# A batch's numerators inside a gate-and-value unit instead of behind it

## The chip, the cores and the metric

The kernel runs on one core of one Trainium2 chip. The metric is the time on the device, in microseconds, from the start to the end of one execution. A run gives one such time; the time of a kernel is the median of several runs. One further execution was taken with the hardware profiler: its span is the time from the first to the last instruction that it recorded. The engines are TensorE (PE, whose weight loads are listed as PEld), VectorE (DVE), ScalarE (ACT), GpSimd (POOL) and SyncE (SP), which here only issues transfers.

## What is computed

An attention with linear cost, and behind it a gated feed-forward block. Cut to what matters, with batch 8, heads 8, sequence 576, head size 64, and 4608 tokens of width 512 in the second part:

```python
def phi(x):                       # cos and sin of a position's angle
    r = np.maximum(x, 0)
    return np.concatenate([r * cos_w, r * sin_w], axis=-1)

q_p, k_p = phi(q), phi(k)         # (b, h, s, 128)
kv  = np.einsum('bhsf,bhsd->bhfd', k_p, v)
z   = k_p.sum(axis=2)
num = np.einsum('bhsf,bhfd->bhsd', q_p, kv)
den = np.einsum('bhsf,bhf->bhs', q_p, z)[..., None] + 1e-6
x   = (num / den).transpose(0, 2, 1, 3).reshape(4608, 512)
g   = x @ w_gate                  # (4608, 1536)
out = (0.5 * g * (1 + erf(g / sqrt(2))) * (x @ w_val)) @ w_out
```

## The kernel before

**The feed-forward part** goes over the tokens in nine blocks: block 0 has the 576 tokens of batch 0, blocks 1 to 7 have 512 each, block 8 has 448. A block's hidden layer of 1536 is cut into 12 units of 128. For each unit, `gate` runs four matmuls of 128x512 (one for each 128 of the width 512) into one PSUM bank, and ScalarE applies the GELU to it; `value` runs four matmuls into another bank, and VectorE multiplies both into `hT`. I call this the product (L233). The gate uses banks 0 and 1 in turn, the value part banks 2 and 3. The output tiles of a block (`o_tile`, twelve matmuls of 128x512 each) run during the next block, behind units 1, 3, 6 and 9, in banks 4 and 5; ScalarE copies the result out and SP stores it.

**The attention of batch n + 1** runs during block n, for n from 1 to 6. Batches 0 and 1 are handled ahead of that, and the change doesn't touch them. In the first units of a block, VectorE and ScalarE scale queries and keys and cast values; a transposing transfer on SP's queue turns the queries (`turn_q`). Then come six steps, `attn_step`, one per unit. Step 0 is the key-value sums: 40 small matmuls into banks 6 and 7 (`kv_half`), which ScalarE copies out to `kv`. Steps 1 to 5 handle 128 tokens each (the last one 64): eight small matmuls of 65 columns, the numerators with their denominators, into banks 6 and 7 (L169); then the normalization on VectorE, which is an addition (L181), a reciprocal (L183) and a multiplication (L184) into the tile `xb`; then a transposing transfer of `xb` into `xT` on SP's queue (`turn_x`, L204). The fifth goes to a tile `xr` first (L207), and POOL copies half of its columns into `xT` (L208). `xT` is what the gates and the value parts read, so a block's last steps feed the next block. Block 2 begins with tokens of batch 1 and reads the first four of batch 2's five parts.

**The order** is written out by hand. The program's order on each engine is the order in which the code issues instructions; nothing reorders them, and an instruction that waits holds up those behind it on its engine or queue. Semaphores are set by the framework from the tiles that instructions read and write. The lists `after[n][unit]` hold what follows a unit: for blocks 2 to 6 the loads of the batch after next stand behind units 3, 4 and 5, step 0 behind unit 5, and steps 1 to 5 behind units 6 to 10. In block 1 all steps are one unit earlier (step 0 behind unit 4, steps 1 to 5 behind units 5 to 9), and the loads stand behind units 5 (queries), 10 (keys) and 11 (values). Output tiles are appended to the same lists last, so behind units 6 and 9 the attention step comes first and the output tile second.

Two consecutive steps use the same two banks: the numerators of a step wait until the normalization of the step before has read them. The key-value sums of step 0 are in the same banks, and the first numerators read their copy, `kv`.

`gv_unit` has a parameter for functions to be called between the gate and the value part. No call in the kernel before uses it.

Of the kernel before, what the change touches and what calls it, by code (L numbers as in the profile page):

```python
# [16 lines left out]
def kernel(  # L17
# [18 lines left out]
    JT = J // 128  # L36
# [9 lines left out]
    NB = len(starts)  # L46
# [166 lines left out]
    def gate(n, jt, c0, w, gb):  # L213

        p0 = starts[n] + c0
        for ct in range(CT):
            nc.tensor.matmul(  # L217
                ps[:, gb, 0:w], lhsT=wg_sb[:, ct, jt * 128:(jt + 1) * 128],
                rhs=xT[:, ct, p0:p0 + w], start=(ct == 0), stop=(ct == CT - 1),
            )  # L220
        gels[n, jt, c0] = gel = rot.tile([128, 512], FP32, name="gel", bufs=3)
        nc.scalar.activation(gel[:, 0:w], ps[:, gb, 0:w], AF.Gelu)  # L222

    def value(n, jt, c0, w, vb):

        p0 = starts[n] + c0
        for ct in range(CT):
            nc.tensor.matmul(  # L228
                ps[:, vb, 0:w], lhsT=wv_sb[:, ct, jt * 128:(jt + 1) * 128],
                rhs=xT[:, ct, p0:p0 + w], start=(ct == 0), stop=(ct == CT - 1),  # L230
            )
        gel = gels.pop((n, jt, c0))
        nc.vector.tensor_mul(hT[n % 2][:, jt, 64 + c0:64 + c0 + w], gel[:, 0:w], ps[:, vb, 0:w])  # L233

    def gv_unit(n, jt, c0, w, gb, vb, mid=()):
        gate(n, jt, c0, w, gb)
        for f in mid:
            f()
        value(n, jt, c0, w, vb)

    def carry(n):

        w = ends[n] - starts[n]
        nc.gpsimd.tensor_copy(hT[(n + 1) % 2][:, :, 0:64], hT[n % 2][:, :, w:w + 64])  # L244
# [205 lines left out]
    def L(f, *a):  # L450
        return lambda: f(*a)
# [70 lines left out]


    after = {n: {jt: [] for jt in range(JT)} for n in range(NB)}
    for n in range(1, 7):
        b = n + 1
        a = after[n]

        def put(u, *fs):
            a[u].extend(fs)  # L530

        s = 0 if n > 1 else -1
        if n > 1:
            put(0, L(sq, 0, 0, "v"), L(sq, 1, 0, "v"), L(sq, 1, 1, "v"), L(sq, 0, 1, "s"))
            put(1, L(sq, 2, 0, "v"), L(sq, 2, 1, "s"), L(turn_q, b, 0, 3))
            put(1, L(sq, 3, 0, "v"), L(sq, 4, 0, "v"), L(sq, 4, 1, "v"), L(sq, 3, 1, "s"), L(turn_q, b, 3, 5))
        else:
            put(0, L(sq, 1, 1, "s"), L(sq, 2, 1, "v"), L(turn_q, b, 0, 3))
            put(0, L(sq, 3, 1, "v"), L(sq, 4, 1, "s"), L(turn_q, b, 3, 5))
        put(2 + s, L(sk, 0, 0, "v"), L(sk, 1, 0, "v"), L(sk, 0, 1, "s"), L(sk, 1, 1, "s"))  # L540
        put(3 + s, L(sk, 2, 0, "v"), L(sk, 3, 0, "v"), L(sk, 4, 0, "v"))
        put(3 + s, L(sk, 2, 1, "s"), L(sk, 3, 1, "s"), L(sk, 4, 1, "s"), L(cast_v, b, 0, 4))
        put(4 + s, L(cast_v, b, 4, 8, "s"))
        put(5 + s, L(attn_step, b, 0))
        if b + 1 < B:

            for f, u in zip((load_q, load_k, load_v), (3, 4, 5) if n > 1 else (5, 10, 11)):
                put(u, L(f, b + 1))
        for i in range(5):
            put(6 + s + i, L(attn_step, b, i + 1))  # L550

    for n in range(2, NB):
        for i, m in enumerate(o_tiles_of(n - 1)):
# [2 lines left out]
    def run_block(n):  # L556
        w = ends[n] - starts[n]
        for jt in range(JT):
            gv_unit(n, jt, 0, w, jt % 2, 2 + jt % 2)
            for f in after[n][jt]:  # L560
                f()
        if n + 1 < NB:
            carry(n)

    for n in range(1, NB):
        run_block(n)
# [34 lines left out]
```

## Time and profile before

| | us |
|---|---|
| median of 9 runs | 328.99 |
| lowest and highest | 328.52, 329.36 |
| the profiled execution's own time | 329.24 |
| its span | 327.1 |
| TensorE busy | 318.7 |
| VectorE busy | 172.4 |
| ScalarE busy | 150.4 |
| POOL busy | 21.3 |
| gate matmuls (L217), 504 | 113.5 |
| value matmuls (L228), 504 | 113.4 |
| output matmuls (L258), 420 | 96.5 |
| numerators (L169), 320 | 16.5 |
| products (L233), 126 | 76.5 |
| normalization's multiplication (L184), 41 | 27.8 |

The granted TensorE clock was 1.000. In a row of the timeline, the first number is the start in us from the beginning of the span, the second the duration in us of the whole group, then engine, line, operation, output and inputs with shapes, and the number of instructions put together. What stands in brackets is the idle time of the engine just before, and what ended it. The ends of matmuls are modelled and neighbours overlap in the records (a group of four of 128x512 lasts 1.03 us, and the next starts 0.86 us after it), so distances are taken from start to start. Rows of waits give the waiting engine, tile and line, what it waited for, the total in us, the number of times, and the longest. A row of SPq is the time that a transfer spent in being issued, not its way to the memory.

### The profile page before, as it was taken

The numbers are of one execution on the slowest core, as the hardware profiler recorded it, in microseconds if no ns is written. First come the engines' busy times: TensorE is split into PE (matmuls) and PEld (weight loads), VectorE is DVE, ScalarE is ACT, GpSimd is POOL, SyncE is SP. The second block draws the span as 40 slices with busy tenths as digits, with TensorE's granted clock in tenths as the row PEclk, the third lists the DMA queues.
The fourth block names the chain that finished last, engine by engine and source line by source line (L and its number), as shares of the span: only waits on it lengthen the run. The fifth ranks groups of instructions, "written<-read, shape, count | busy, mean of one in ns | idle before, by whom it ended". The sixth has DMA issues, their size and how long they took to land.

```text
span 327.1 us, 5862 instructions
## 1 busy us (share of the span) xinstructions
PE 318.7 (97%) x2222; PEld 167.2 (51%) x2222; DVE 172.4 (53%) x383; ACT 150.4 (46%) x269; POOL 21.3 (7%) x41
## 2 busy tenths in 40 slices
PE   7899999999999999999999999999999999999994
PEld 3587866554445444544454445444544444444443
DVE  4895676868753667364835484547455222322210
ACT  5664664772574256424652375237622332223321
POOL 2550010000100010001000010001000100100000
PEclk9999999999999999999999999999999999999999
DMA  7999999897799938993699459994623211000024
GB/s 227 284 205 273 214 305 298 312 182 168 203 273 288 279 86 154 299 272 80 127 308 275 96 98 191 371 146 83 146 49 81 43 37 34 32 32 32 34 65 96
DMA packets 87739, 55.42 MB, mean 169 GB/s; under 512 B 52512, under 2 KB 82976, under 8 KB 87712
## 3 DMA queue, kind: packets, MB, share of 16 engines
q1 hardware_dynamic: 81200, 48.71, 60.1%
q0 software_dynamic: 6080, 5.90, 10.1%
q10 hardware_dynamic: 432, 0.46, 0.4%
q8 instruction: 17, 0.28, 0.3%
q14 instruction: 10, 0.08, 0.1%
HBM read 37.75 MB, written 9.44 MB: 144 GB/s over the span
## 4 chain that ended last, share of the span: by engine, by line
PE 92%; DVE 3%; DMA 2%; issue 1%; ACT 0%; POOL 0%; SPq 0%; DVEq 0%; POOLq 0%; ACTq 0%
PE ps L217 28%; PE ps L228 28%; PE ps L258 28%; PE ps L169 3%; PE ps L153 3%; DMA qf<-in_q_dram 2%; PE ps L323 1%; DVE hT L233 1%; PE ps L276 1%; PE ps L342 1%; DVE xb L184 1%; DVE vx L140 0%; SPq L79 0%; DVE qp L134 0%; DVE rec L183 0%
## 5 line engine op out<-in xcount | busy, mean ns | idle before, releaser
L233 DVE TENSOR_TENSOR hT<-gel,ps 128x512 bf16<-128x512 f32 (+5 forms) x126 | 76.5, 610 | 128.4 <-PE ps L228 124.7
L228 PE MATMUL ps<-xT,wv_sb 128*128 128x512 bf16 (+5 forms) x504 | 113.4, 349 | 0.8 <-DVE hT L233 0.8
L217 PE MATMUL ps<-xT,wg_sb 128*128 128x512 bf16 (+5 forms) x504 | 113.5, 348 | 0.2
L222 ACT ACTIVATE gel<-ps 128x512 f32<-128x512 f32 (+5 forms) x126 | 67.5, 536 | 77.6 <-PE ps L217 75.3
L258 PE MATMUL ps<-wo_sb,hT 128*128 128x512 bf16 x420 | 96.5, 379 | 0.0
L228 PEld LDWEIGHTS <-wv_sb 128*128 128x128 bf16 x504 | 47.9, 98 | 47.1 <-issue 1.0
L217 PEld LDWEIGHTS <-wg_sb 128*128 128x128 bf16 x504 | 45.7, 98 | 40.6 <-DVE xT L345 0.4
L258 PEld LDWEIGHTS <-hT 128*128 128x128 bf16 x420 | 40.0, 98 | 45.4
L287 ACT COPY o_sb<-ps 128x512 f32<-128x512 f32 x35 | 20.5, 585 | 75.4 <-PE ps L258 72.3
L184 DVE TENSOR_TENSOR xb<-ps,rec 128x512 bf16<-128x512 f32 (+2 forms) x41 | 27.8, 678 | 1.7 <-DVE rec L183 0.2
L136 ACT ACTIVATE kp<-kf,sin_c 128x512 bf16<-128x512 f32 (+1 forms) x41 | 25.4, 681 | 0.9 <-DMA kf<-in_k_dram 0.9
L134 DVE TENSOR_SCALAR qp<-qf,cos_c 128x512 bf16<-128x512 f32 x40 | 20.3, 549 | 0.0
L169 PEld LDWEIGHTS <-qT 128*128 128x128 bf16 (+1 forms) x320 | 15.0, 98 | 9.1 <-issue 2.3
L134 DVE TENSOR_SCALAR kp<-kf,cos_c 128x512 bf16<-128x512 f32 (+1 forms) x45 | 18.7, 463 | 1.5 <-DMA kf<-in_k_dram 1.5
L136 ACT ACTIVATE qp<-qf,sin_c 128x512 bf16<-128x512 f32 x28 | 19.2, 712 | 0.0
L169 PE MATMUL ps<-kv,qT 128*128 128x65 bf16 (+1 forms) x320 | 16.5, 193 | 0.5 <-DVE xb L184 0.3
L208 POOL COPY xT<-xr 128x256 bf16<-128x256 bf16 x6 | 2.4, 400 | 200.4 <-DMA xr<-xb 200.4
L153 PEld LDWEIGHTS <-kp 128*128 128x128 bf16 x320 | 10.9, 97 | 2.6 <-issue 0.7
L126 PE MATMUL ps<-junk 128*128 128x512 bf16 x34 | 10.5, 460 | 1.7 <-DVE par_i L103 1.7
L153 PE MATMUL ps<-vx,kp 128*128 128x65 bf16 x320 | 11.1, 193 | 0.1
L140 ACT CAST vx<-vf 128x1280 bf16<-128x1280 f32 (+1 forms) x9 | 9.7, 1076 | 1.2 <-DMA vf<-in_v_dram 1.2
L244 POOL COPY hT<-hT 128x768 bf16<-128x768 bf16 x8 | 7.6, 946 | 37.8 <-DVE hT L233 37.8
(55 smaller groups left out, 88.4 us busy)
## 6 DMA issues: line engine op xcount, KB each, us to landing
out_dram<-o_sb SPq DMA_DIRECT2D x38, 128.0 KB, 2.4
kf<-in_k_dram SPq DMA_DIRECT2D x7, 640.0 KB, 7.0
out_dram<-o_sb SPq DMA_DIRECT2D x16, 256.0 KB, 3.1
qf<-in_q_dram SPq DMA_DIRECT2D x6, 640.0 KB, 6.0
vf<-in_v_dram SPq DMA_DIRECT2D x6, 640.0 KB, 10.0
kf<-in_k_dram SPq DMA_DIRECT2D x7, 512.0 KB, 5.9
qf<-in_q_dram SPq DMA_DIRECT2D x6, 512.0 KB, 4.5
vf<-in_v_dram SPq DMA_DIRECT2D x6, 512.0 KB, 8.3
```

The source lines that it names most:

```text
L126: nc.tensor.matmul(ps[:, bank, :], lhsT=junk[:, 0:128], rhs=junk, start=True, stop=True)
L134: nc.vector.tensor_scalar(d, s, col, 0.0, op0=ALU.mult, op1=ALU.max)
L136: nc.scalar.activation(d, s, AF.Relu, scale=col)
L153: nc.tensor.matmul(ps[:, bank, (h % 4) * (D + 1):(h % 4 + 1) * (D + 1)], lhsT=kp[:, j, h, :], rhs=vx[b % 2][:, j, h, 0:D + 1], start=(j == ...
L169: nc.tensor.matmul(ps[0:rows, bank + g, (h % 4) * (D + 1):(h % 4 + 1) * (D + 1)], lhsT=qT[b % 2][:, t, h, 0:rows], rhs=kv[b % 2][:, h, 0:D ...
L184: nc.vector.tensor_tensor(xb[0:rows, g0:g1], nd[:, :, :, 0:D], rec[0:rows, 0:n, :, None].to_broadcast([rows, n, 4, D]), op=ALU.mult,)
L217: nc.tensor.matmul(ps[:, gb, 0:w], lhsT=wg_sb[:, ct, jt * 128:(jt + 1) * 128], rhs=xT[:, ct, p0:p0 + w], start=(ct == 0), stop=(ct == CT - 1),
L222: nc.scalar.activation(gel[:, 0:w], ps[:, gb, 0:w], AF.Gelu)
L228: nc.tensor.matmul(ps[:, vb, 0:w], lhsT=wv_sb[:, ct, jt * 128:(jt + 1) * 128], rhs=xT[:, ct, p0:p0 + w], start=(ct == 0), stop=(ct == CT - 1),
L233: nc.vector.tensor_mul(hT[n % 2][:, jt, 64 + c0:64 + c0 + w], gel[:, 0:w], ps[:, vb, 0:w])
L258: nc.tensor.matmul(ps[:, bank, :], lhsT=hT[n % 2][:, jt, c0:c0 + 128], rhs=wo_sb[:, jt, :], start=(jt == 0), stop=(jt == JT - 1),)
L287: nc.scalar.copy(o_sb, ps[:, bank, :])
```

## The change

The steps that compute numerators (1 to 5 of each batch, in blocks 1 to 6) are taken out of the lists of what follows a unit and put into new lists, `mid`, for the same unit. `gv_unit` calls them behind its gate and ahead of its value part. Step 0, the loads, the scaling and the output tiles stay in the lists of what follows. With a step, everything that it issues moves: the eight matmuls, the three VectorE operations, the transposing transfer on SP's queue, and POOL's copy in the fifth step.

```diff
     after = {n: {jt: [] for jt in range(JT)} for n in range(NB)}
+
+    mid = {n: {jt: [] for jt in range(JT)} for n in range(NB)}
     for n in range(1, 7):
...
         for i in range(5):
-            put(6 + s + i, L(attn_step, b, i + 1))
+            mid[n][6 + s + i].append(L(attn_step, b, i + 1))
...
         for jt in range(JT):
-            gv_unit(n, jt, 0, w, jt % 2, 2 + jt % 2)
+            gv_unit(n, jt, 0, w, jt % 2, 2 + jt % 2, mid[n][jt])
             for f in after[n][jt]:
                 f()
```

The variable `s` is -1 in block 1 and 0 in the others. On VectorE the order in such a unit was product, then L181, L183, L184; it becomes L181, L183, L184, then product. On SP's queue nothing changes its place against anything else but in block 1: there, unit 5 holds both the query load of batch 3 and the first transpose of batch 2. The load was first; now the transpose is first.

## The prediction

> **What bounds the kernel now.** I read the page's totals and chain first, then who waits on TensorE, then the timeline of the units that the diff touches.
>
> ```profile
> span 327.1 us, 5862 instructions
> ...
> PE 318.7 (97%) x2222; PEld 167.2 (51%) x2222; DVE 172.4 (53%) x383; ACT 150.4 (46%) x269; POOL 21.3 (7%) x41
> ...
> PE 92%; DVE 3%; DMA 2%; issue 1%; ACT 0%; POOL 0%; SPq 0%; DVEq 0%; POOLq 0%; ACTq 0%
> ```
>
> ```profile
> PE ps L228 <- DVE hT L233: 0.8, 2, 0.6
> ...
> PE ps L169 <- DVE xb L184: 0.3, 1, 0.3
> ```
>
> TensorE is the chain. What can be gained is only the time in which it stands still, and the modelled ends hide most of that: L169 (the numerators) shows 0.3 us. So I go by starts. The next shows two units of block 4.
>
> ```profile
> 168.45 1.02 PE L217 MATMUL ps<-xT,wg_sb 128*128 128x512 bf16 x4
> 168.65 0.38 ACT L165 CAST kv<-ps 128x260 bf16<-128x260 f32 x1 [0.23 <-PE ps L153]
> ...
> 169.32 1.03 PE L228 MATMUL ps<-xT,wv_sb 128*128 128x512 bf16 x4
> ...
> 175.01 1.02 PE L217 MATMUL ps<-xT,wg_sb 128*128 128x512 bf16 x4
> 175.02 0.69 DVE L233 TENSOR_TENSOR hT<-gel,ps 128x512 bf16<-128x512 f32 x1 [2.85 <-PE ps L228]
> 175.63 0.16 DVE L181 TENSOR_SCALAR den<-ps 128x8 f32<-128x8 f32 x1
> ...
> 175.87 1.03 PE L228 MATMUL ps<-xT,wv_sb 128*128 128x512 bf16 x4
> 176.06 0.69 DVE L184 TENSOR_TENSOR xb<-ps,rec 128x512 bf16<-128x512 f32 x1
> ...
> 176.80 0.41 PE L169 MATMUL ps<-kv,qT 128*128 128x65 bf16 x8
> ```
>
> Gate (L217) to value (L228) is 175.01 to 175.87: 0.86 us for four matmuls. The value part should end at 175.87 + 0.86 = 176.73, and the numerators start at 176.80: 0.07 us lost. They write the banks that the normalization before them (L181, L183, L184) still reads; its last operation ends at 176.06 + 0.69 = 176.75, and the numerators follow 0.05 us later. The same difference, start of the numerators minus start of the value part minus 0.86, taken over all 30 numerator steps of blocks 1 to 6, is above 0.03 us seven times: 0.45 (at 74.55 us) and 0.07 in block 1, 0.08 in block 2, 0.27 in block 3 (at 143.18), and 0.07 in each of blocks 4, 5 and 6. **Sum 1.08 us.** Between 60 and 320 us I find no other stop of TensorE above 0.03 us.
>
> The two large ones:
>
> ```profile
> 72.77 0.69 DVE L233 TENSOR_TENSOR hT<-gel,ps 128x512 bf16<-128x512 f32 x1 [2.24 <-PE ps L169]
> 73.24 1.03 PE L228 MATMUL ps<-xT,wv_sb 128*128 128x512 bf16 x4
> ...
> 73.80 0.69 DVE L184 TENSOR_TENSOR xb<-ps,rec 128x512 bf16<-128x512 f32 x1
> ...
> 74.55 0.41 PE L169 MATMUL ps<-kv,qT 128*128 128x65 bf16 x8 [0.28 <-DVE xb L184]
> ...
> 142.43 0.69 DVE L184 TENSOR_TENSOR xb<-ps,rec 128x512 bf16<-128x512 f32 x1 [0.23 <-DVE rec L183]
> ```
>
> Here VectorE itself was late: a product (L233) starts 1.13 us after its value part starts in nearly every unit, but 1.51 at 72.77 (value part at 71.26), so 0.38 us late; at 142.43 the normalization is 0.19 us late, and at 213.03 a product 0.35 us, which stopped nobody. They lie some 70 us and 88 VectorE instructions apart.
>
> **The change, step by step.** No instruction is added or removed; thirty steps (eight matmuls, three VectorE operations, one transposing DMA each, and a POOL copy in the fifth of a batch) go ahead of four value matmuls and a product.
>
> *TensorE.* The same matmuls. A numerator step takes 0.25 us between its neighbours' starts (174.75 to 175.01), in either place: 0.
>
> *The wait on the normalization.* Count from the start of a gate. Before: value part ends at 1.73, product at 1.73 + 0.27 = 2.00 (1.13 less 0.86), L181 at 2.61 (175.02 to 175.63), last read at 2.61 + 1.12 = 3.73 (175.63 to 176.75), released at 3.79; the next numerators are due at 1.98 + 1.73 = 3.71. Late by 0.08: the row's 0.07. The next step, itself delayed, is in time again, hence one loss per pair of neighbouring units without an output tile between. After: numerators end at 0.86 + 0.25 = 1.11, L181 at 1.38 if this release costs 0.27 too, last read at 2.50, release 2.56; next numerators due at 1.98 + 0.86 = 2.84. **Slack 0.28 instead of -0.08.** The product is now late: ready at 2.25, it starts at 1.81 + 0.61 = 2.42 (L184 starts 0.43 after L181, and the operation behind it 0.61 later); VectorE is free at 3.03, L181 comes at 3.36. A product's bank is wanted two units later: nobody waits. All 1.08 us go if no other stall comes.
>
> *VectorE's odd delays.* They seem to belong to a place in the instruction stream. The row says 0.38, 0.19 and 0.35 us. The Trainium skill (Runtime: NRT & Kernel Launch, "Instruction fetch mechanics") says that engines refill their instructions in blocks and that crossing a boundary is "mostly hidden"; that these rows are such crossings is my guess: no row names them, but a packet of the instruction queue q14 follows each within 8 us (at 76 to 77, 146 to 150, 214 to 215 us). By the rule nothing is left to pay; by the rows the first delay falls, at the same count, on block 1's first normalization: L181 due at 71.26 + 0.25 + 0.27 = 71.78, normalization over at 72.90 + 0.38 = 73.28, released 73.34, next numerators due at 73.24: 0.10 lost. The second falls on a product, the third on a step with an output tile behind: 0. I take 0.05, from 0 to 0.4.
>
> *The wait on the key-value sums.* The first numerators of a batch now follow those sums by a gate alone. ScalarE's copy runs 168.65 to 169.03, the gate ends at 169.31: slack 0.28, less about 0.06 for the release. Cost 0, covered by that gate; behind it in TensorE's queue stands everything. If the copy came 0.3 us later it would cost 0.1 in each of 6 blocks.
>
> *SP's queue.* From block 2 on, the loads stand in units 3 to 5 and the output tiles remain behind the step: the order is unchanged, and each transpose is some 1.2 us earlier. In block 1 the first step shares unit 5 with the next batch's query load. It was behind the load; now the load stands behind the transpose, which waits for the normalization.
>
> ```profile
> 70.20 1.89 SPq L79 DMA_DIRECT2D qf<-in_q_dram  x2
> ...
> 80.53 1.24 SPq L204 DMA_TRANSPOSE xT<-xb  x1
> ```
>
> The Trainium skill (DMA: Bandwidth & Descriptors, "Rules for kernel authors") says to issue a DMA early and wait late, and this speaks against the change: the load moves from 70.20 to about 74.2 (transpose issued at 72.9, 1.2 us in the queue). The load landed 6.3 us after issue, so about 80.5; the query scaling of block 2 wants it at about 85: hidden. The rule's price would be the 4 us only if that cover were gone. But the transposes now run behind the load. The fourth (L204) is what block 2's first gate reads. Before, it is issued at 80.53 and lands some 3.2 us later (median of two in 72 to 78 us), 83.7, for a gate at 84.27. After, its normalization ends at 78.85; behind the load, which holds the engines to about 80.5, and two transposes of about 0.8 us each (the DMA slices at 79.7 to 80.5 and 81.7 to 82.5), it lands at about 82.7, for a gate at 83.75: slack 1. Cost 0; the longest landing of such a transpose in the trace, 9.3 us, would cost 4.4.
>
> POOL's copy (0.40 us) is earlier, its order with the carry is kept: 0. The later keys and values stand behind the fifth transpose and so are issued earlier, not later.
>
> *Sum.* -1.08 + 0.05 = -1.03 us. The profiled execution took 329.24 us (span 327.1), so 328.21. The median of the runs, 328.99, is 0.25 below it; I take the same gain from that: **328.0 us**.
>
> **Rivals.**
> 1. *Gain realized*: 327.7 to 328.3. For it: the same sum reproduces the 0.07 of the old order. Against it: two thirds of the gain (0.45 + 0.27) come from delays whose cause I don't know.
> 2. *Only the regular stops go*: VectorE's delays strike a normalization again. The gain is 1.08 - 0.72 = 0.36 (five times 0.07 to 0.08): 328.6, too little to tell from nothing. For it: the delays recur by count; against it: the slack of 0.28 swallows most of one.
> 3. *Slower: block 2 starts without its fourth transpose*, because the query load now stands ahead of it in SP's queue. It decides from a landing at 83.75 on; at 84.8 it has eaten the gain, and 6.9 us after issue (halfway to 9.3; 85.8) costs 2.0: 330.0. For it: transposes with loads in flight took 4.01 us in SP's queue at 104.76; against it: there three loads were ahead, here one.
> 4. *The key-value copy becomes the wait*: 0.22 slack, six times. Copy and release would have to be 0.4 us longer to cost 6 x 0.18 = 1.1, which cancels the gain: 329.0.
>
> **How the numbers follow.** Chances: rival 1 60%, 2 17%, 3 13%, 4 6%, and 4% for what I haven't seen, mostly slower. A change of this kernel under 0.2% (0.66 us) can't be told from none. Faster is rival 1 and a little of the second: 0.62. Same is the rest of rivals 2 and 4: 0.21. Slower: 0.17. The likeliest case alone spans 327.7 to 328.3. The range goes from 327.5 (all stops gone and the scatter of the nine runs, 0.4 below their median) up through rivals 2 and 4 to 329.6, where rival 3 begins; what is left out is that rival and what is unseen.
>
> **What would show it.** Right: value part and numerators follow gate and numerators without a gap at all 30 steps; L181 follows the numerators ahead of L233; the wait of L169 on L184 is gone. Rival 2: one numerator step in block 1 still some tenths late. Rival 3: a gap ahead of block 2's first gate, near 83.8 us, released by a DMA into xT. Rival 4: the first numerators of each batch start over 0.86 us after their gate. The prediction is wrong if TensorE's stops stay near 1 us in sum wherever they lie, or if a matmul costs more in the new order.

## The result, and the profile after

The changed kernel takes **327.83 us** (median of 10 runs, 327.30 to 328.48) against 328.93 for the kernel before (30 runs beside it): a ratio of 0.9967, with a 95% interval from 0.9959 to 0.9975. That is 1.10 us less; the prediction was 328.0, 0.99 us below the median that it started from (1.03 in the sum, rounded). The profiled execution took 327.84 us, with a span of 325.7 instead of 327.1.

Totals and chain of the changed kernel, from its page:

```profile
span 325.7 us, 5868 instructions
...
PE 318.1 (98%) x2222; PEld 167.2 (51%) x2222; DVE 169.8 (52%) x383; ACT 150.5 (46%) x269; POOL 20.6 (6%) x41
...
PE 94%; DVE 2%; DMA 2%; issue 1%; ACT 0%; DVEq 0%
```

The waits of TensorE in the changed kernel (waiting line, what it waited for, us in total, times, longest):

```profile
...
PE ps L228 <- DVE hT L233: 0.8, 2, 0.6
PE ps L217 <- DMA xT<-xb: 0.3, 1, 0.3
```

The numerators' wait for the normalization (L169 on L184) is gone. A new wait has come: a gate on a transposing transfer. The timeline of the same two units of block 4 as shown for the kernel before:

```profile
167.67 0.38 ACT L165 CAST kv<-ps 128x260 bf16<-128x260 f32 x1 [0.23 <-PE ps L153]
168.34 0.42 PE L169 MATMUL ps<-kv,qT 128*128 128x65 bf16 x8
...
173.80 0.69 DVE L184 TENSOR_TENSOR xb<-ps,rec 128x512 bf16<-128x512 f32 x1
...
174.03 1.03 PE L217 MATMUL ps<-xT,wg_sb 128*128 128x512 bf16 x4
174.41 0.68 DVE L233 TENSOR_TENSOR hT<-gel,ps 128x512 bf16<-128x512 f32 x1
...
174.89 0.42 PE L169 MATMUL ps<-kv,qT 128*128 128x65 bf16 x8
...
175.15 1.02 PE L228 MATMUL ps<-xT,wv_sb 128*128 128x512 bf16 x4
175.34 0.17 DVE L181 TENSOR_SCALAR den<-ps 128x8 f32<-128x8 f32 x1 [0.26 <-PE ps L169]
```

The numerators start 0.86 us after their gate (174.03 to 174.89): no loss. The first of the batch start at 168.34, 0.29 us after ScalarE's copy ends (167.67 + 0.38); that wait costs nothing. L181 comes 0.45 us after the start of its numerators, and VectorE now waits for TensorE, not the other way round.

By the count used in the prediction (distance from start to start, less the work in between) TensorE's stops in blocks 1 to 6 fell from 1.08 to 0.12 at the numerators. The two places where something is left, in block 1 and ahead of block 2:

```profile
70.56 0.42 PE L169 MATMUL ps<-kv,qT 128*128 128x65 bf16 x8
...
71.46 0.17 DVE L181 TENSOR_SCALAR den<-ps 128x8 f32<-128x8 f32 x1 [1.64 <-ACT gel L222]
...
71.67 1.03 PE L217 MATMUL ps<-xT,wg_sb 128*128 128x512 bf16 x4
...
72.65 0.42 PE L169 MATMUL ps<-kv,qT 128*128 128x65 bf16 x8
...
82.29 1.03 PE L228 MATMUL ps<-xT,wv_sb 128*128 128x512 bf16 x4
...
83.61 1.02 PE L217 MATMUL ps<-xT,wg_sb 128*128 128x512 bf16 x4 [0.29 <-DMA xT<-xb]
```

L181 at 71.46 is 0.90 us behind its numerators instead of 0.45: VectorE's odd delay has moved onto the normalization, and the next numerators start 0.98 us after their gate, 0.12 late. At 83.61 block 2's first gate is 0.46 us late (82.29 + 0.86 = 83.15), waiting for the fourth transpose.

The span can be taken apart in every trace into four parts: the time until block 1's first gate, these stops, the time from the start of the last tile's matmuls (L276) to the end (from the unrounded span), and the rest. The rest is 258.31 to 258.36 us in all fourteen traces, so the other three explain every difference. In the traces of the experiments some matmul records are missing; a hole of one matmul (0.216 us) at such a place is not counted.

| kernel | until block 1 | stops at numerators | stop ahead of block 2 | last tile to end | span | median time |
|---|---|---|---|---|---|---|
| before | 60.56 | 1.08 | 0 | 7.14 | 327.1 | 328.93 |
| before, again | 60.34 | 1.07 | 0 | 7.16 | 326.9 | (one run: 329.06) |
| changed | 59.86 | 0.12 | 0.46 | 6.90 | 325.7 | 327.83 |
| changed, again | 61.28 | 0.11 | 0.07 | 6.90 | 326.7 | 327.70 |
| block 1 alone | 60.24 | 0.44 | 0.12 | 7.33 | 326.5 | 328.70 |
| blocks 2 to 6 alone | 60.07 | 0.52 | 0 | 6.90 | 325.8 | 327.97 |
| before, two more | 60.21 | 0.70 | 0 | 6.89 | 326.1 | 328.25 |
| changed, two more | 60.26 | 0 | 0.07 | 6.91 | 325.6 | 327.72 |
| changed, load first | 60.26 | 0.11 | 0 | 6.90 | 325.6 | 327.65 |
| changed, load first, two more | 60.23 | 0 | 0 | 6.91 | 325.5 | 327.66 |
| before, second reciprocal | 60.25 | 0.87 | 0 | 6.90 | 326.4 | 328.42 |
| changed, second reciprocal | 60.30 | 0.09 | 0.41 | 6.91 | 326.1 | 327.98 |
| before, longer normalization | 60.27 | 2.32 | 0 | 6.91 | 327.8 | 329.93 |
| changed, longer normalization | 60.07 | 0.32 | 0.22 | 6.91 | 325.9 | 328.18 |

So the 1.4 us between the first two profiled spans are 0.70 of start, 0.50 of stops and 0.24 of end. The start is not the change's: its instructions are the same, and it went from 59.86 to 61.28 with the changed kernel alone.

### The profile page after: what moved, and what is told of

Read it like the earlier page. It is cut to its first block, busy times and chain, and to the rows that moved or that the text cites. A ratio compares the mean times of both kernels' runs of the same rounds, so it can differ in the third digit from the quotient of the medians.

```text
span 325.7 us, 5868 instructions
## 1 busy us (share of the span) xinstructions
PE 318.1 (98%) x2222; PEld 167.2 (51%) x2222; DVE 169.8 (52%) x383; ACT 150.5 (46%) x269; POOL 20.6 (6%) x41
## 4 chain that ended last, share of the span: by engine, by line
PE 94%; DVE 2%; DMA 2%; issue 1%; ACT 0%; DVEq 0%
PE ps L217 28%; PE ps L258 28%; PE ps L228 28%; PE ps L169 3%; PE ps L153 3%; PE ps L126 2%; DMA xT<-xb 2%; PE ps L323 1%; PE ps L276 1%; PE ps L342 1%; DVE hT L233 0%; DVE vx L140 0%; DVE qp L134 0%; DVE qT L331 0%; DVE xb L184 0%
## 5 line engine op out<-in xcount | busy, mean ns | idle before, releaser
L233 DVE TENSOR_TENSOR hT<-gel,ps 128x512 bf16<-128x512 f32 (+5 forms) x126 | 76.2, 608 | 89.5 <-PE ps L228 88.7
L217 PEld LDWEIGHTS <-wg_sb 128*128 128x128 bf16 x504 | 47.0, 98 | 45.8 <-issue 0.9
L228 PEld LDWEIGHTS <-wv_sb 128*128 128x128 bf16 x504 | 45.9, 98 | 40.0 <-issue 1.0
L258 PEld LDWEIGHTS <-hT 128*128 128x128 bf16 x420 | 40.8, 98 | 47.7
L181 DVE TENSOR_SCALAR den<-ps 128x8 f32<-128x8 f32 (+2 forms) x41 | 6.8, 165 | 43.1 <-PE ps L169 41.5
L184 DVE TENSOR_TENSOR xb<-ps,rec 128x512 bf16<-128x512 f32 (+2 forms) x41 | 27.8, 678 | 1.5
L169 PEld LDWEIGHTS <-qT 128*128 128x128 bf16 (+1 forms) x320 | 15.0, 98 | 8.2 <-issue 0.6
L134 DVE TENSOR_SCALAR qp<-qf,cos_c 128x512 bf16<-128x512 f32 x40 | 17.8, 489 | 0.0
L169 PE MATMUL ps<-kv,qT 128*128 128x65 bf16 (+1 forms) x320 | 16.6, 194 | 0.1
```

Source lines behind the costliest of these rows:

```text
L134: nc.vector.tensor_scalar(d, s, col, 0.0, op0=ALU.mult, op1=ALU.max)
L169: nc.tensor.matmul(ps[0:rows, bank + g, (h % 4) * (D + 1):(h % 4 + 1) * (D + 1)], lhsT=qT[b % 2][:, t, h, 0:rows], rhs=kv[b % 2][:, h, 0:D ...
L184: nc.vector.tensor_tensor(xb[0:rows, g0:g1], nd[:, :, :, 0:D], rec[0:rows, 0:n, :, None].to_broadcast([rows, n, 4, D]), op=ALU.mult,)
L217: nc.tensor.matmul(ps[:, gb, 0:w], lhsT=wg_sb[:, ct, jt * 128:(jt + 1) * 128], rhs=xT[:, ct, p0:p0 + w], start=(ct == 0), stop=(ct == CT - 1),
L228: nc.tensor.matmul(ps[:, vb, 0:w], lhsT=wv_sb[:, ct, jt * 128:(jt + 1) * 128], rhs=xT[:, ct, p0:p0 + w], start=(ct == 0), stop=(ct == CT - 1),
L258: nc.tensor.matmul(ps[:, bank, :], lhsT=hT[n % 2][:, jt, c0:c0 + 128], rhs=wo_sb[:, jt, :], start=(jt == 0), stop=(jt == JT - 1),)
```

## The experiments

**The kernel before, traced again.** No edit.

> The kernel before once more, for a second trace: the seven stops stand at the same places with the same sizes within 0.03 us (0.45, 0.07, 0.08, 0.27, 0.07, 0.07, 0.07) if they belong to the order of instructions. The start of block 1 (60.6 us in the first trace, 59.9 in that of the changed kernel) shows if those 0.7 us vary from run to run.

The stops are at the same seven places: 0.44, 0.07, 0.08, 0.27, 0.07, 0.07, 0.07, in sum 1.07. The late operations on VectorE are the same three (L233 at 72.54, L184 at 142.20, L233 at 212.80). The stops belong to the order of instructions. The start was 0.22 us shorter.

**Block 1 alone, and the other blocks alone.**

```diff
-            mid[n][6 + s + i].append(L(attn_step, b, i + 1))
+            (mid[n][6 + s + i] if n == 1 else a[6 + s + i]).append(L(attn_step, b, i + 1))
```

> Numerators inside the unit in block 1 alone. Stops: 0.12 + 0.46 in and behind block 1, and the old ones of blocks 2 to 6 (0.08 + 0.27 + 3 x 0.07 = 0.56), in sum 1.14 us against 1.08 before: 329.0 us, no gain. If the gain came with each moved step whatever the stops say, a fifth of 1.1 us: 328.7.

Measured: 328.70 us (13 runs), ratio 1.0000 (0.9992 to 1.0009). No gain, as the stops said, though their sum is 0.56, not 1.14: block 3's 0.27 became 0.07 without that block being touched (VectorE's delay was no longer seen there), and the gate ahead of block 2 lost 0.12. The end took 7.33 us, 0.19 longer than before, which gives back part of the 0.5.

```diff
-            mid[n][6 + s + i].append(L(attn_step, b, i + 1))
+            (mid[n][6 + s + i] if n > 1 else a[6 + s + i]).append(L(attn_step, b, i + 1))
```

> Numerators inside the unit in blocks 2 to 6 alone. The stops of these blocks (0.56 us) go, block 1's old ones (0.45 + 0.07) stay, the gate of block 2 doesn't wait: 328.93 - 0.56 = 328.4 us. If the gain came with each moved step, five sixths of 1.1: 328.0.

Measured: 327.97 us (9 runs), ratio 0.9976 (0.9967 to 0.9986), so 0.8 us gained. The stops of blocks 2 to 6 are gone (0.56), block 1's are there (0.45 + 0.07), block 2's gate doesn't wait; the end is 0.24 shorter than in the first trace of before. 0.56 + 0.24 = 0.80 is what was measured; the expected 328.4 left out the end.

**The two stops that were left: the load's place in SP's queue.**

```diff
-            for f, u in zip((load_q, load_k, load_v), (3, 4, 5) if n > 1 else (5, 10, 11)):
+            for f, u in zip((load_q, load_k, load_v), (3, 4, 5) if n > 1 else (4, 10, 11)):
```

> The changed kernel with the query load of batch 3 put behind block 1's unit 4, so that it stands ahead of the first transpose in SP's queue, as before the change; all else as changed. If the transposes behind that load are what stops block 2's first gate (0.46 us in the profile of the changed kernel), that stop goes, block 1's 0.12 us stays, and the time falls from 327.83 to about 327.4 us. If the stop has another cause (the transposes or TensorE's earlier arrival alone), it stays and the time is 327.8.

The stop ahead of block 2 is gone and block 1's 0.11 stays, so there is no such stop without the load's new place. The landing of the fourth transpose (last number, us from its issue) in this kernel, from the transfers issued between 78 and 79.5 us:

```profile
xT<-xb SPq DMA_TRANSPOSE x1, 2.5
```

and in the changed kernel, between 78 and 79 us:

```profile
xT<-xb SPq DMA_TRANSPOSE x1, 5.1
```

It is issued at 78.62 and 78.22 us and lands at 81.1 and 83.4. The time, 327.65 us (5 runs; ratio 0.9968, 0.9956 to 0.9981), is 0.18 below the changed kernel's, inside both intervals: the end of this stop isn't resolved in the time.

**VectorE's delay: a place in the instruction stream?** Two tiny memsets on VectorE at about 5 us, where it waits for a load.

```diff
     nc.vector.tensor_mul(sin_c[:, NJ:NJ + 1], sin_c[:, NJ:NJ + 1], even)
+    pad = sb.tile([1, 8], FP32, name="pad")
+    [nc.vector.memset(pad[:, i:i + 1], 0.0) for i in range(2)]
```

> The kernel before with two tiny memsets more on VectorE at about 5 us, where it waits for a load. If VectorE's delay belongs to a count of instructions, it moves two instructions back, from the product of block 1's unit 5 to that of unit 4, which waits for ScalarE in any case: the 0.45 us stop falls to 0.1 or less, time about 328.5 us. If it belongs to a time, a transfer or the product itself, the product of unit 5 is 0.38 late again: 328.9.

Two units of block 1 in this kernel:

```profile
71.13 0.81 PE L228 MATMUL ps<-xT,wv_sb 128*128 128x512 bf16 x3
71.77 0.42 PE L169 MATMUL ps<-kv,qT 128*128 128x65 bf16 x8
...
72.05 0.69 DVE L233 TENSOR_TENSOR hT<-gel,ps 128x512 bf16<-128x512 f32 x1 [1.86 <-PE ps L228]
...
72.89 1.03 PE L228 MATMUL ps<-xT,wv_sb 128*128 128x512 bf16 x4
...
73.82 0.42 PE L169 MATMUL ps<-kv,qT 128*128 128x65 bf16 x8
```

The product follows the end of its value part as in any other unit, and the next numerators are 0.07 late (72.89 + 0.86 = 73.75) instead of 0.45. The sum of stops is 0.70, the time 328.25 us (12 runs; ratio 0.9980, 0.9971 to 0.9988). Two instructions that do nothing made the kernel before 0.6 us faster: 0.37 by the stops, 0.25 by the end.

> The changed kernel with the same two memsets. By the count, L181 of block 1's first step is in time (0.46 us behind the start of its numerators, not 0.90), and the 0.12 us stop goes. The stop ahead of block 2 stays between 0.1 and 0.5, since the load behind the first transpose starts 0.4 earlier: about 327.6 us. If the delay doesn't follow the count: L181 late as before, 327.8.

```profile
70.96 0.42 PE L169 MATMUL ps<-kv,qT 128*128 128x65 bf16 x8
...
71.48 0.17 DVE L181 TENSOR_SCALAR den<-ps 128x8 f32<-128x8 f32 x1 [1.25 <-PE ps L169]
```

L181 is 0.52 us behind the start of its numerators, not 0.90, and the 0.12 stop is gone; 0.07 is left ahead of block 2. The time is 327.72 us (5 runs; ratio 0.9958, 0.9946 to 0.9971). Both edits follow the count.

So do the places themselves. Counted in the order of the trace's VectorE records, with the waits for semaphores that the timeline leaves out, the late instructions of the kernel before are number 192, 320, 448 and 576, each 128 behind the last. In the kernel with a second reciprocal, where VectorE gets through more instructions in the same time, they are again 192, 320, 448 and 576, at 72.46, 136.68, 200.99 and 285.29 us. Number 576 of the kernel before is the last but one of its 577, at the very end of the program.

The two kernels with the memsets are also the fairest comparison of the two orders, since their ends are equal (6.89 and 6.91 us) and number 192 stops TensorE in neither: 328.25 against 327.72, 0.53 us, with 0.70 us of stops against 0.07. (0.20 of the 0.70 is still a normalization that number 448 delays; the two intervals just touch.) So about half of the 1.10 us is the order's own gain here, and the rest went with where VectorE's delays fall.

**Both at once**, the load first and the two memsets:

> The changed kernel with the query load of batch 3 behind unit 4 and two tiny memsets more on VectorE. If the two stops that are left (0.12 and 0.46) have the causes given, none above 0.05 us remains between 62 and 280 us: 327.3 us, about 0.5 below the changed kernel. If the last stops are worth nothing in the end: 327.7.

No stop above 0.04 us is left between 62 and 280 us, and the span, 325.5 us, is the shortest of all. But the time, 327.66 us (5 runs; ratio 0.9969, 0.9956 to 0.9981), is the changed kernel's within the error: traced again on the same chip beside it, that one has 327.70. The gain from these last stops can't be told from none.

**The margin.** First a second reciprocal that nobody reads, in each of the 30 normalizations:

```diff
         nc.vector.reciprocal(rec[0:rows, 0:n], den[0:rows, 0:n])
+        rec2 = rot.tile([128, 2, 4], FP32, name="rec2")
+        nc.vector.reciprocal(rec2[0:rows, 0:n], den[0:rows, 0:n])
```

> The kernel before with a second reciprocal in each of the 30 normalizations in blocks 1 to 6, its result unused: VectorE needs about 0.24 us more a step. If the margin of the numerators is -0.08 us before the change, the seven small losses grow to about 0.3 each, and the sum of stops from 1.08 to some 2.6 us: 330.5 us. If what counts is VectorE's work in sum, 30 x 0.24 = 7 us spread over idle time, nothing in particular: below 329.2.

> The changed kernel with the same second reciprocal. The margin by the trace is 0.34 us (last read ends 174.49, next numerators 174.89, release 0.06), less 0.24 leaves 0.1: no new stop in blocks 2 to 6, in block 1 the step with VectorE's delay loses 0.24 more (0.12 to 0.36): 328.1 us. If the new order had no margin of its own it would lose as much as the old one: 329.4.

The expectation for the kernel before failed: 328.42 us (13 runs; ratio 0.9984, 0.9976 to 0.9992), faster than without. The added operation ran in the 0.24 us between the start of L183 and that of L184, which waits for the first reciprocal, so the normalization was no longer; and the 30 instructions moved VectorE's second delay off block 3's normalization (0.27 became 0.07) and its fourth away from the end (7.14 became 6.90). The changed kernel took 327.98 us (8 runs; ratio 0.9970, 0.9960 to 0.9980). As a test of the margin it told nothing. So the multiplication was made to read a copy of the reciprocal:

```diff
         nc.vector.reciprocal(rec[0:rows, 0:n], den[0:rows, 0:n])
+        rec2 = rot.tile([128, 2, 4], FP32, name="rec2")
+        nc.vector.tensor_copy(rec2[0:rows, 0:n], rec[0:rows, 0:n])
         nc.vector.tensor_tensor(
             xb[0:rows, g0:g1], nd[:, :, :, 0:D],
-            rec[0:rows, 0:n, :, None].to_broadcast([rows, n, 4, D]), op=ALU.mult,
+            rec2[0:rows, 0:n, :, None].to_broadcast([rows, n, 4, D]), op=ALU.mult,
         )
```

> The kernel before with one operation more between the reciprocal and the multiplication of each of the 30 normalizations: the multiplication reads a copy of the reciprocal, so the normalization ends about 0.24 us later. (A second reciprocal that nobody reads cost nothing: it ran in the 0.24 us in which the multiplication waits for the first.) With a margin of -0.08 us, the first of two neighbouring steps in each of blocks 2 to 6 loses about 0.32 us instead of 0.08, and block 1 about 0.69 + 0.32: sum of stops about 2.6 us against 1.08, time 330.4 us. If the margin is not what stops TensorE: 328.9.

The timeline of block 4 in the kernel before, so lengthened:

```profile
176.20 1.03 PE L228 MATMUL ps<-xT,wv_sb 128*128 128x512 bf16 x3
176.39 0.17 DVE L183 COPY rec<-rec 128x8 f32<-128x8 f32 x1
176.60 0.69 DVE L184 TENSOR_TENSOR xb<-ps,rec 128x512 bf16<-128x512 f32 x1
...
177.34 0.41 PE L169 MATMUL ps<-kv,qT 128*128 128x65 bf16 x8
```

Value part to numerators is now 1.14 us, of which 0.28 is lost: the multiplication ends at 177.29, and the numerators go 0.05 later. The copy costs 0.21 us a step. Each of blocks 2 to 6 loses 0.28, block 1 0.64 + 0.28, in sum 2.32 us; the time is 329.93 us (5 runs; ratio 1.0033, 1.0020 to 1.0046), slower than before by 1.1.

> The changed kernel with the same longer normalization. A margin of 0.34 us less 0.24 leaves 0.1: no stop in blocks 2 to 6; in block 1, 0.36 at the step that VectorE's delay strikes, and 0.4 ahead of block 2: sum about 0.8, time 328.1 us. If the new order had no more margin than the old, the sum is 2 us or more and the time over 329.3.

The same in the changed kernel:

```profile
174.19 0.69 DVE L184 TENSOR_TENSOR xb<-ps,rec 128x512 bf16<-128x512 f32 x1
174.21 1.03 PE L217 MATMUL ps<-xT,wg_sb 128*128 128x512 bf16 x4
174.79 0.68 DVE L233 TENSOR_TENSOR hT<-gel,ps 128x512 bf16<-128x512 f32 x1
175.07 0.42 PE L169 MATMUL ps<-kv,qT 128*128 128x65 bf16 x8
```

The multiplication ends at 174.88 and the numerators follow their gate in 0.86 us. There is no stop in blocks 2 to 6, 0.32 in block 1 and 0.22 ahead of block 2: 328.18 us (17 runs; ratio 0.9980, 0.9973 to 0.9987). The same longer normalization costs the old order 1.25 us of stops and the new order none outside block 1. The margin is shown.

**The changed kernel, again.**

> The changed kernel once more, timed beside the others and traced a second time: stops 0.12 and 0.3 to 0.5, the time from the start of the last tile's matmuls to the end 6.9 us (7.1 to 7.2 in both traces of the kernel before) if that belongs to the kernel, 327.8 us.

Measured: 327.70 us (12 runs; ratio 0.9971, 0.9962 to 0.9979). The stops are 0.11 and 0.07; the profiled execution began late (61.28 us), waiting for the first query load, and is the slowest of its twelve. The end takes 6.88 us.

## Why the prediction was right

*The wait on the normalization, -1.08.* Right, in place and size. All seven stops went where the steps moved (block 1 apart), and the lengthened normalization shows that it is the margin that decides: -0.08 before, and enough to take 0.21 more after. The predicted slack of 0.28 was a little low: L184 ends at 173.80 + 0.69 = 174.49 in the changed kernel, and the numerators start at 174.89, which leaves 0.34 after 0.06 for the release. The release of L181 by the numerators takes less than the 0.27 assumed.

*VectorE's odd delays, +0.05.* The first place was right and the arithmetic too: 0.10 worked out, 0.12 and 0.11 measured; the halving to 0.05 was not needed. The second and third were placed by counting VectorE's work alone. The changed kernel has six instructions more (5868 against 5862), all of them VectorE's waits for semaphores, though the prediction says that none is added; with these, numbers 320 and 448 are waits behind a reciprocal (140.02 and 209.12 us), and no operation behind them is late. That the delay goes by the count of instructions is shown by the two memsets, and at such a place the cost is not "mostly hidden", as the rule of the Trainium skill that the prediction weighed has it (Runtime: NRT & Kernel Launch, "Instruction fetch mechanics"), if these are the crossings that it means. That it is the refill of instructions is still not shown. For it: a packet of 8,192 bytes of the queue q14 follows each late instruction of the kernel before within 0.6 to 3.8 us, and 8,192 is 64 bytes for each of 128 instructions. But it begins after the late instruction, so it is not what that one waited for.

*The key-value sums, 0.* Right. The first numerators of a batch follow their gate at once.

*SP's queue, 0.* This step failed. The fourth transpose was to land about 1 us ahead of block 2's first gate, and it lands 0.07 to 0.46 us too late in all six traces in which the load stands behind the first transpose. The mechanism is rival 3's, at a fraction of its price.

The load itself was not the term that was off. The prediction took it to be through at about 80.5 on the time axis of the kernel before; in the changed kernel its last data packet ends at 79.89, which is 80.6 on that axis, since block 1 began 0.70 earlier. (The sum got there by luck: 6.3 us is the landing time of the load's second transfer, and it was added to the issue of the first.) What was put at nothing is an instruction packet that comes next, in the queue q8. From the changed kernel's transfers between 79 and 80 us, and its DMA share in 40 slices from 80 to 84 us:

```profile
q8 instruction: 1, 0.02, 6.3%
DMA  3999090000000001039997999999999961635458
```

This packet has 16,384 bytes, begins at 79.99 and takes 1.00 us. Of the transposes, 24 packets of 256 bytes begin between 80.25 and 80.54 and stay open until 81.77 to 81.82, 1.5 us for what takes about 0.02 otherwise. The view books a packet where it begins, so its zeros are no rest: these packets are open all the while. Then the three transposes behind the load land at 82.4, 82.9 and 83.4. Without that 1.5 us the fourth would land at about 81.9, over 1 us ahead of its gate (an estimate: 83.4 less 1.5).

In each of the fourteen traces such a packet begins between 77.6 and 80.6 us, and packets of a transpose stay open until 0.7 to 0.9 us after its end. With the load first it strikes the third transpose, which then lands 3.6 to 4.3 us after its issue, and the fourth is in time; with the load behind the first transpose, three are waiting at once. That the instruction packet is what holds them up is read from this agreement, and no run moved the packet alone. That there is no stop without the load's new place is shown by the run with the load first.

*What was not in the sum.* The end is 0.24 to 0.26 us shorter in both traces of the changed kernel than in both of the one before. This is VectorE's delay again, at number 576. In the kernel before, that is the last instruction of the kind DRAIN in VectorE's records: it starts 0.47 and 0.46 us after the wait ahead of it, against 0.09 in the eleven traces in which neither of the two is number 576. With block 1 alone, 576 is that wait itself, 0.41 us late, and the end takes 7.33 us. The two memsets take 576 away from there, and the end takes 6.89. So the changed kernel gained a quarter of a microsecond because six more waits moved the count, not because of its order: luck, as far as the prediction goes.

So the total is right partly by balance. Stops gave -0.50 us in one pair of traces and -0.89 in the other, the end -0.24 and -0.26: -0.74 and -1.15, against a measured change of 0.82 to 1.35 by the interval (and 0.69 to 1.25 in the later comparison).

## What to carry to other kernels

Where TensorE is always busy, look at who must be done before a small step may start, and count both orders from start to start: moving a dependent step half a unit earlier cost nothing here and turned a margin of -0.08 us into +0.34. When a step is moved, check each queue that its last instruction goes through: with the load behind one transpose, the next three ran late together, and an instruction packet met all of them instead of one. And differences of a few tenths of a microsecond can come from where an engine's instruction count stands, so take the trace apart before crediting an edit with them, and compare two orders once more with a few idle instructions in both.

## What was unexpected

- VectorE is about 0.4 us late at fixed numbers of its instruction stream (192, 320, 448, 576, waits included), 0.19 where the late one follows a reciprocal closely, and not at all where it would wait for something else anyway. Two idle memsets moved the kernel before from 328.87 to 328.25 us.
- Transposing transfers behind a load of 640 and 512 KB took 5.1 to 7.1 us to land in the changed kernel, instead of 2.4 to 2.5. Some 1.5 us of this followed a single instruction packet of 16 KB.
- A VectorE operation added between a reciprocal and the operation that waits for it took no time: 0.24 us lie between their starts, of which the reciprocal itself is 0.20.
